# A long convolution with experts on one core: a Fourier transform without the filter's zero taps, and the experts' second product with its weights stationary

## The chip, the cores and the metric

The kernel runs on one core of a Trainium2 chip. The metric is device time in microseconds. The engines are TensorE (PE; its weight loads are shown as PEld), VectorE (DVE), ScalarE (ACT), GpSimd (POOL) and SyncE (SP), which here only issues DMAs. Each engine takes its instructions in the order in which they are written in the program; engines wait for one another by semaphores.

## The reference

There are B = 2 sequences of S = 12480 tokens with D = 128 channels. A small network makes a filter from position embeddings, a window exp(-0.01 pos) damps it, and the product u = x * v is convolved with it causally along the tokens (by a Fourier transform of length 2 S). The result times x goes, token by token, through experts of 2048 hidden units with a rational function.

```python
h_filt = (np.maximum(pos_emb @ w1, 0.0) @ w2) * np.exp(-0.01 * pos)[:, None]
u = x * v
y = irfft(rfft(u, n=2 * S) * rfft(h_filt, n=2 * S))[:, :S]
x = (x * y).reshape(B * S, D)
h = x @ w_in                                   # (24960, 2048)
P = a[0] + a[1] * h + a[2] * h**2 + a[3] * h**3
Q = 1.0 + abs(b[0]) * abs(h) + abs(b[1]) * h**2
out = (P / (Q + 1e-6)) @ w_out                 # (24960, 128)
```

All data are float32 (w_in, w_out and the scalars arrive as float64 and are converted in the kernel).

## The kernel before

A token n is written as n = 128 m + n2: 98 blocks m of 128 residues n2. The transform of length L = 24960 = 195 * 128 is taken in two stages, for some channels at a time: over the blocks m for each residue (s1, a matmul with f1, to K1 = 98 frequencies), a rotation by twiddles on VectorE and GpSimd, then over the residues (s2, with dft). There the spectrum is multiplied with the filter's, and s3 goes back over the residues (with idft). The last step back, from the K1 frequencies to the blocks m, is done later, per residue, in attn_a (with the constants g).

**First part.** The filter network runs over groups of residues (hf_w, hf_t, hf_1, hf_2; 98 rows m each), and meanwhile the expert weights are converted. Then a loop over 32 groups of CG = 4 channels makes the filter's spectrum (stored to h_d) and the convolution of batch 0 (stored to y_d). Per group VectorE makes two products of 784 elements for the filter's twiddles (L160, L161), four sums of 392 (L543 to L546), two products of 784 for the input's twiddles (L160, L161) and two for the spectrum (L192, L193); GpSimd makes the sums of these (L166, L167, L195, L196) and ys (L568, L569).

**Second part.** The tokens are taken in 52 tiles of 5 residues (490 tokens; the last tile of each half batch has 4 residues, 392 tokens). A tile has four steps (c = 0 to 3) of 4 blocks of 128 hidden units (NWF = 4). In a step s the work of several steps is in flight, in this written order (from the loop at L987):

```python
run(s, act_q, 0); run(s, act_v, 0); run(s + 1, mm1, 0); run(s - 2, dve_e); slot(s, 0)
run(s, dve_v, 0); run(s, act_q, 1); run(s - 1, act_ln); run(s - 3, mm2); run(s - 2, dve_n); slot(s, 1)
run(s, act_v, 1); run(s, act_sq); run(s + 1, mm1, 1); run(s, dve_v, 1); run(s - 1, act_exp); run(s - 2, dve_g); slot(s, 2)
```

mm1 is the first product (two halves of 6 passes in fast float32, L844 to L846). ScalarE makes q (L854) and v (L863) from its result in PSUM, per half, then a square of q (L887), a logarithm (L891) and an exponential (L894) over whole steps. VectorE makes v (L873) per half and, over whole steps, e (L899), n (L904) and g (L908). mm2 (L922) is the second product: the tokens' values g are the stationary side, 128 tokens at a time, and the rows of w_out move, so that the sums come out with the tokens on the partitions, 4 chunks by 4 blocks a step. At the end of a tile store copies the sums from PSUM (L933, L936) and issues some 8 DMAs (L944).

Beside that, each call of slot places one further matmul group on TensorE: attn_a (half a tile's residues: the last step back of the transform, then x times it on VectorE, L796), attn_b (transposes, then ScalarE's ahi, L814, and VectorE's alo, L815, the input of the next tile) or, in the free slots, the next step of batch 1's convolution, two channels at a time: s1 (taken up by L154 on VectorE, then L166, L167 on GpSimd), s2 (L188, then L195, L196), s3 (ScalarE's L205). What a slot's matmuls made is taken up (take_up) only in the next call of slot, and all share one PSUM buffer (cv). A tile has 12 slots; ATTN gives those for attn_a, attn_a, attn_b: (1, 2, 4) beside the convolution, (1, 3, 5) without. The free slots take s1, s2, s3 in turn.

The product u for batch 1 is made by GpSimd (L230) in four quarters of 32 channels, 8 pieces each, two pieces per slot (load_step); all quarters use one buffer, so that a quarter begins after the last s1 of the one before. READY says how many slots after the last piece s1 may begin: 5 for the first quarter, 2 for the others. GpSimd first clears two rows (L225).

## Time and profile before

| | before |
|---|---|
| median of 3 runs | 2547.77 us (2546.77 to 2547.78) |
| span of the profiled execution | 2545.4 us |
| profiled execution's own time | not listed apart from its span; the median lies 2.4 us above the span |
| VectorE busy | 2411.3 us, 95% |
| TensorE busy, its weight loads | 2180.8 us, 86%; 1829.2 us, 72% |
| ScalarE busy | 2103.6 us, 83% |
| GpSimd busy | 561.5 us, 22% |
| second product L922 | 6656 passes, 833.2 us busy |

The engines' busy time over the span, in 40 equal slices of 64 us, each digit a share in tenths (9 is 90% or more):

```
DVE  8999997799999998999899999999999999999997
ACT  6311121899999997999899999999999999999996
POOL 3466656222242224124321200000000000000000
```

The first seven slices are the first part, the next sixteen have batch 1's convolution beside the experts (GpSimd's work ends with it), the rest are experts alone. In the timeline rows below the first number is the start in us from the beginning of the span, the second the duration; then engine, line, operation, output and inputs, shapes, count, and in brackets how long the engine was idle before and for whom it waited. Instructions of one engine overlap a little in the records, so that the distance between two starts says better than the duration what an instruction costs a full engine.

### The profile page before, as it was taken

How to read it: one execution, taken by the hardware profiler on the slowest of the kernel's cores; microseconds unless marked ns; L12 is line 12 of the kernel's file. 1: busy time of each engine (PE TensorE's matmuls, PEld its weight loads, DVE VectorE, ACT ScalarE, POOL GpSimd, SP SyncE). 2: the span in 40 equal slices, each digit the busy share in tenths (PEclk: the TensorE clock that was granted, in tenths of full speed). 3: DMA queues.
4: the chain of work that ended last, by engine and by line, in shares of the span. 5: the costliest groups of instructions: out<-in, count | busy, mean ns of one | idle time of the engine just before them, and what ended most of it. 6: DMA issues, size and time to landing. Idle time of an engine off the chain costs nothing.

```text
span 2545.4 us, 33926 instructions
## 1 busy us (share of the span) xinstructions
PE 2180.8 (86%) x13344; PEld 1829.2 (72%) x13344; DVE 2411.3 (95%) x1945; ACT 2103.6 (83%) x1919; POOL 561.5 (22%) x522
## 2 busy tenths in 40 slices
PE   6888888789989998999899989888888898888877
PEld 4666665678877877788788767667776777776665
DVE  8999997799999998999899999999999999999997
ACT  6311121899999997999899999999999999999996
POOL 3466656222242224124321200000000000000000
PEclk9999989899999999999999999999999999999999
DMA  7444422822162235222322121111111111111100
GB/s 157 95 112 112 112 74 98 139 68 61 44 117 54 53 68 99 55 73 46 72 75 53 49 49 45 32 40 31 44 44 22 41 44 44 45 30 31 40 11 13
DMA packets 366001, 158.68 MB, mean 62 GB/s; under 512 B 299508, under 2 KB 347256, under 8 KB 362696
## 3 DMA queue, kind: packets, MB, share of 16 engines
q1 hardware_dynamic: 358696, 130.56, 23.2%
q10 hardware_dynamic: 7136, 25.86, 3.1%
q8 instruction: 107, 1.75, 0.3%
q14 instruction: 62, 0.51, 0.1%
HBM read 105.06 MB, written 51.31 MB: 61 GB/s over the span
## 4 chain that ended last, share of the span: by engine, by line
ACT 34%; DVE 30%; PE 21%; issue 9%; POOL 2%; DMA 1%; SPq 1%; ACTq 0%; DVEq 0%; POOLq 0%
ACT r L891 9%; ACT r L894 9%; ACT q L854 8%; PE acc L922 7%; DVE v L908 6%; ACT v L863 5%; DVE r L904 3%; DVE q L899 3%; PE cv L201 3%; PE cv L202 2%; DVE ta L188 2%; DVE v L873 2%; DVE tb L161 2%; PE cv L142 2%; DVE zh L544 2%
## 5 line engine op out<-in xcount | busy, mean ns | idle before, releaser
L922 PE MATMUL acc<-wout,v 128*128 128x128 f32 (+2 forms) x6656 | 833.2, 284 | 59.2 <-DVE v L908 35.2
L922 PEld LDWEIGHTS acc<-wout,v 128*128 128x128 f32 (+2 forms) x6656 | 790.6, 193 | 111.4 <-DVE v L908 55.3
L863 ACT ACTIVATE v<-h,sc 128x980 f32<-128x980 f32 (+1 forms) x416 | 683.2, 1642 | 8.0 <-PE acc L922 8.0
L854 ACT ACTIVATE q<-h 128x980 f32<-128x980 f32 (+1 forms) x416 | 613.7, 1559 | 6.4 <-PE h L846 6.4
L873 DVE SCALAR_TENSOR_TENSOR v<-v,sc,h 128x980 f32<-128x980 f32 (+1 forms) x416 | 504.9, 1214 | 59.7 <-ACT v L863 57.6
L887 ACT ACTIVATE q<-q,sc 128x1960 f32<-128x1960 f32 (+1 forms) x208 | 516.2, 2482 | 0.0
L891 ACT ACTIVATE r<-q,sc 128x1960 f32<-128x1960 f32 (+1 forms) x208 | 515.0, 2476 | 0.2 <-DVE v L908 0.2
L894 ACT ACTIVATE r<-r 128x1960 f32<-128x1960 f32 (+1 forms) x208 | 497.1, 2390 | 0.0
L899 DVE SCALAR_TENSOR_TENSOR q<-q,sc,r 128x1960 f32<-128x1960 f32 (+1 forms) x208 | 467.3, 2247 | 4.9 <-ACT r L894 1.1
L908 DVE SCALAR_TENSOR_TENSOR v<-v,sc,r 128x1960 f32<-128x1960 f32 (+1 forms) x208 | 465.5, 2238 | 0.1
L844 PE MATMUL h<-ahi,win_l 128*128 128x490 f32 (+1 forms) x832 | 365.0, 439 | 100.9 <-DVE v L873 98.5
L904 DVE SCALAR_TENSOR_TENSOR r<-q,r 128x1960 f32<-128x1960 f32 (+1 forms) x208 | 450.7, 2167 | 0.1
L845 PE MATMUL h<-alo,win_h 128*128 128x490 f32 (+1 forms) x832 | 320.6, 385 | 0.0
L846 PE MATMUL h<-ahi,win_h 128*128 128x490 f32 (+1 forms) x832 | 318.1, 382 | 0.0
L844 PEld LDWEIGHTS h<-ahi,win_l 128*128 128x128 f32 x832 | 158.5, 191 | 158.8 <-DVE v L873 133.3
L195 POOL TENSOR_TENSOR yy<-ta 128x196 f32<-128x196 f32 x64 | 122.1, 1908 | 368.3 <-DVE ta L188 368.3
L846 PEld LDWEIGHTS h<-ahi,win_h 128*128 128x128 f32 x832 | 158.7, 191 | 26.4
L845 PEld LDWEIGHTS h<-alo,win_h 128*128 128x128 f32 x832 | 159.4, 192 | 16.0 <-DVE alo L815 0.4
L790 PE MATMUL cv<-yc,gt 98*98 98x128 f32 x1004 | 130.9, 277 | 32.4 <-DVE an L796 29.9
L790 PEld LDWEIGHTS cv<-yc,gt 98*98 98x98 f32 x1004 | 115.0, 165 | 52.1 <-DVE an L796 48.6
L205 ACT ACTIVATE ys<-cv 98x512 f32<-98x512 f32 x64 | 76.9, 1202 | 76.2 <-PE cv L202 76.2
L201 PE MATMUL cv<-idft,yy 128*98 128x256 f32 x256 | 80.6, 396 | 57.3 <-DVE ta L188 33.1
(109 smaller groups left out, 2574.5 us busy)
## 6 DMA issues: line engine op xcount, KB each, us to landing
yc<-y_d SPq DMA_DIRECT2D x23, 980.0 KB
gt<-in_g_dram SPq DMA_DIRECT2D x48, 375.2 KB
h_d<-hg ACTq DMA_DIRECT2D x32, 392.0 KB
y_d<-ys ACTq DMA_DIRECT2D x16, 784.0 KB
hg<-h_d SPq DMA_DIRECT2D x64, 196.0 KB
y_d<-ys SPq DMA_DIRECT2D x16, 784.0 KB
xq<-in_x_dram SPq DMA_DIRECT2D x32, 196.0 KB
vq<-in_v_dram SPq DMA_DIRECT2D x32, 196.0 KB
```

The lines of the kernel that those rows point to most:

```text
L844: nc.tensor.matmul(out=t[:, k, 0:w], lhsT=wl, rhs=hi[:, 0:w], start=True, stop=False)
L845: nc.tensor.matmul(out=t[:, k, 0:w], lhsT=wh, rhs=lo[:, 0:w], start=False, stop=False)
L854: nc.scalar.activation(out=halves(st_q[s], i, width(s)), in_=st_h[s, i], func=AF.Abs, **({} if short else {"scale": col("b0")}))
L863: nc.scalar.activation(out=v, in_=st_h[s, i], func=AF.Square, bias=col("s"))
L873: stt(out=v, in0=v, scalar=col("k"), in1=h, op0=ALU.add, op1=ALU.mult)
L887: nc.scalar.activation(out=whole(st_q, s), in_=whole(st_q, s), func=AF.Square, bias=col("dl"))
L891: nc.scalar.activation(out=whole(st_r, s), in_=whole(st_q, s), func=AF.Ln, **({"bias": col("ka")} if short else {}))
L894: nc.scalar.activation(out=whole(st_r, s), in_=whole(st_r, s), func=AF.Exp, scale=-1.0)
L899: nc.vector.scalar_tensor_tensor(out=q, in0=q, scalar=col("ka") if short else 0.0, in1=whole(st_r, s), op0=ALU.add, op1=ALU.mult)
L904: nc.vector.scalar_tensor_tensor(out=r, in0=whole(st_q, s), scalar=2.0, in1=r, op0=ALU.subtract, op1=ALU.mult)
L908: nc.vector.scalar_tensor_tensor(out=v, in0=v, scalar=col("p0" if short else "a0"), in1=whole(st_r, s), op0=ALU.add, op1=ALU.mult)
L922: nc.tensor.matmul(out=acc[j][0:k, q // 128, :], lhsT=g[:, i, q:q + k], rhs=wout[:, f, :], start=(f == 0 and q == 0), stop=(f == NF - 1), ...
```

## The change

The window exp(-0.01 n) is zero in float32 from token 10398 on, so that many filter taps are left out. With TAPS = 10398 the filter has MF = 82 blocks for 98, the transform's length need only be S + TAPS - 1, which gives N1 = 179 blocks for 195, L = 22912, and K1 = 90 frequencies for 98. All tiles with K1 in their shape shrink by that; the filter network runs over 82 rows. The loads of pos_emb are cut in rows 0 to 79 and 80, 81.

In mm2 a block of w_out is now stationary and the step's 490 tokens move, so that the sums come out with the channels on the partitions (one bank of 490 columns). mm2 is called in two halves. At the tile's end collect copies the sums to SBUF; two slots of the next tile (o0 and o1) transpose them back, 3 and 2 residues at a time, and their takes copy them from PSUM by ScalarE; after the second two DMAs store the tile, with the 5 residues of a block of tokens side by side (2560 bytes). A step has four slots; SLOTS gives what stands in the 16 of a tile, and two ("") stay empty. The loads for the tile after next are asked for in slot 8.

```diff
-L = 2 * S
-N1 = L // N2
-K1 = 98
+WINDOW = np.exp(np.float32(-0.01) * np.arange(S, dtype=np.float32))
+TAPS = int(np.flatnonzero(WINDOW)[-1]) + 1
+MF = min(M, -(-TAPS // N2))
+N1 = -(-(S + TAPS - 1) // N2) // 2 * 2 + 1
+L = N1 * N2
+K1 = (N1 + 1) // 2
...
-ATTN = ((1, 2, 4), (1, 3, 5))
+SLOTS = ({1: "a0", 3: "a1", 5: "b", 8: "", 11: "", 13: "o0", 15: "o1"},
+         {1: "a0", 4: "a1", 7: "b", 13: "o0", 15: "o1"})
...
-            load_rows(t[:, 0:NPL], pos_emb, H2 + p0, NPL, 0, FO, True)
-            load_rows(t[:, NPL:], pos_emb, H2 - p0 - NPL, NPL, 0, FO, True)
+            for o, t0 in ((0, H2 + p0), (NPL, H2 - p0 - NPL)):
+                    for r0, r1 in ((0, MF // 16 * 16), (MF // 16 * 16, MF)):
+                        nc.sync.dma_start(out=t[r0:r1, o:o + NPL], in_=rows(pos_emb, r0, r1 - r0, t0, NPL, 0, FO))
...
-        def mm2(s):
-                acc[j] = accp.tile([128, 4, D], F32, tag="acc", name="acc")
-            for i in range(NWF):
-                f = NWF * c + i
-                for q in range(0, w, 128):
-                    k = min(128, w - q)
-                    nc.tensor.matmul(out=acc[j][0:k, q // 128, :], lhsT=g[:, i, q:q + k], rhs=wout[:, f, :], ...)
+        def mm2(s, i):
+                acc[j] = accp.tile([128, 512], F32, tag="acc", name="acc")
+            for k in range(2 * i, 2 * i + 2):
+                f = NWF * c + k
+                nc.tensor.matmul(out=acc[j][:, 0:w], lhsT=wout[:, f, :], rhs=st_v[s][:, k, 0:w], ...)
...
-        def store(j):
-            nc.scalar.activation(out=t[:, 0:full, :], in_=a[:, 0:full, :], func=AF.Identity)
-                nc.scalar.activation(out=t[0:k, full, :], in_=a[0:k, full, :], func=AF.Identity)
-            while p < w:
-                    nc.sync.dma_start(out=ob[...], in_=t[...])
+        def collect(j):
+            ot[j] = mp.tile([128, NPT * M], F32, tag="ot", name="ot", bufs=1)
+            nc.scalar.activation(out=ot[j][:, 0:w], in_=acc.pop(j)[:, 0:w], func=AF.Identity)
+        def store(j, q):
+            def fill(cv):
+                for i in range(i0, i1):
+                    nc.tensor.transpose(out=cv[0:M, 0, (i - i0) * D:(i - i0 + 1) * D], in_=t[:, i * M:(i + 1) * M],
+                                        identity=ident)
+            def take(cv):
+                nc.scalar.activation(out=o[:, i0:i1, :].rearrange("p t c -> p (t c)"),
+                                     in_=cv[0:M, 0, 0:(i1 - i0) * D], func=AF.Identity)
+                if i1 == n:
+                    for r0, r1 in ((0, 96), (96, M if n0 < H2 else M - 1)):
+                        nc.sync.dma_start(out=..., in_=o[r0:r1, 0:n])
+            issue(fill, take)
...
+            what = at.get(i)
+            if what:
+                t = j - 1 if what[0] == "o" else j + 1
+                if 0 <= t < len(tiles):
+                    (store if what[0] == "o" else attn_a)(t, q) if what[1:] else attn_b(t)
+                    return
             take_up()
-            if i == at[2] + 1:
+            if i == 8:
                 load_xg(j + 2)
                 load_y(j + 2)
-            conv_step((i - sum(i > k for k in at)) % 3)
+            if what is None:
+                conv_step((i - sum(i > k for k in at)) % 3)
...
             run(s - 1, act_ln)
-            run(s - 3, mm2)
+            run(s - 3, mm2, 0)
+            slot(s, 1)
             run(s - 2, dve_n)
-            slot(s, 1)
             run(s, act_v, 1)
+            run(s - 3, mm2, 1)
+            slot(s, 2)
             run(s, act_sq)
             run(s + 1, mm1, 1)
             run(s, dve_v, 1)
             run(s - 1, act_exp)
             run(s - 2, dve_g)
-            slot(s, 2)
+            slot(s, 3)
             if s >= 3 and steps[s - 3][1] == NC - 1:
-                store(steps[s - 3][0])
+                collect(steps[s - 3][0])
+        for q in range(2):
+            store(len(tiles) - 1, q)
+        take_up()
```

## Rows read from the trace of the kernel before

**Rows 1.** Busy time by stretch: length, PE, PEld, DVE, ACT, POOL, clock, DMA
```profile
80.00:240.00 160.00, 134.56 (x637) 99.87 (x636) 156.74 (x177) 29.32 (x50) 97.38 (x83) 0.97 0.46 109
...
446.00:1481.00 1035.00, 932.70 (x5928) 809.22 (x5928) 967.72 (x667) 938.28 (x789) 304.30 (x291) 0.98 0.32 69
1489.00:2478.00 989.00, 830.55 (x5409) 710.05 (x5407) 974.20 (x621) 989.00 (x838) 0.00 (x0) 0.97 0.15 37
```

**Rows 2.** Timeline of ScalarE in the late stage, one tile
```profile
2441.84 2.33 ACT L933 ACTIVATE ot<-acc 128x384 f32<-128x384 f32 x1
2442.21 2.13 ACT L936 ACTIVATE ot<-acc 106x128 f32<-106x128 f32 x1
2442.37 2.85 ACT L854 ACTIVATE q<-h 128x980 f32<-128x980 f32 x1
...
2478.84 2.48 ACT L933 ACTIVATE ot<-acc 128x384 f32<-128x384 f32 x1
```

**Rows 3.** Timeline of ScalarE beside the convolution
```profile
854.38 0.57 ACT L814 ACTIVATE ahi<-cv 128x490 fp32r<-128x490 f32 x1
...
880.85 1.22 ACT L205 ACTIVATE ys<-cv 98x512 f32<-98x512 f32 x1 [0.99 <-PE cv L202]
881.84 1.04 ACT L854 ACTIVATE q<-h 128x980 f32<-128x980 f32 x1
882.78 1.92 ACT L891 ACTIVATE r<-q,sc 128x1960 f32<-128x1960 f32 x1
884.60 1.06 ACT L863 ACTIVATE v<-h,sc 128x980 f32<-128x980 f32 x1
885.56 1.92 ACT L887 ACTIVATE q<-q,sc 128x1960 f32<-128x1960 f32 x1
...
889.11 0.97 ACT L854 ACTIVATE q<-h 128x980 f32<-128x980 f32 x1
...
898.14 0.57 ACT L814 ACTIVATE ahi<-cv 128x490 fp32r<-128x490 f32 x1
```

**Rows 4.** Timeline of VectorE beside the convolution
```profile
877.82 0.97 DVE L188 TENSOR_TENSOR ta<-cv,hg 128x784 f32<-128x784 f32 x1
878.71 2.25 DVE L899 SCALAR_TENSOR_TENSOR q<-q,sc,r 128x1960 f32<-128x1960 f32 x1
880.87 1.23 DVE L873 SCALAR_TENSOR_TENSOR v<-v,sc,h 128x980 f32<-128x980 f32 x1
882.02 2.19 DVE L904 SCALAR_TENSOR_TENSOR r<-q,r 128x1960 f32<-128x1960 f32 x1
...
885.69 1.24 DVE L873 SCALAR_TENSOR_TENSOR v<-v,sc,h 128x980 f32<-128x980 f32 x1 [0.59 <-ACT v L863]
886.84 2.25 DVE L908 SCALAR_TENSOR_TENSOR v<-v,sc,r 128x1960 f32<-128x1960 f32 x1
889.01 0.55 DVE L796 TENSOR_TENSOR an<-cv,xt 98x384 f32<-98x384 f32 x1
```

**Rows 5.** Timeline of TensorE beside the convolution
```profile
878.85 0.67 PE L201 MATMUL cv<-idft,yy 128*98 128x256 f32 x2 [0.78 <-DVE ta L188]
...
882.89 3.72 PE L922 MATMUL acc<-wout,v 128*128 128x128 f32 x32
```

**Rows 6.** Groups by line: busy us, mean ns of one, idle before
```profile
L160 DVE TENSOR_TENSOR ta<-cs,tw 128x784 f32<-128x784 f32 x32 | 31.2, 974 | 1.1 <-POOL zu L167 0.2
L543 DVE TENSOR_TENSOR zh<-ta,tb 64x392 f32<-64x392 f32 x32 | 41.2, 1287 | 1.1
```

**Rows 7.** Timeline of TensorE in the first part, passes of 392 columns
```profile
319.33 0.82 PE L177 MATMUL cs<-zu,dft 128*128 128x392 f32 x2
319.99 0.82 PE L178 MATMUL cs<-zu,dft 128*128 128x392 f32 x2
```

**Rows 8.** Timeline of GpSimd and TensorE at the change to the third quarter
```profile
948.00 1.80 POOL L225 MEMSET uq<- 2x2048 f32 x1 [6.99 <-PE cv L142]
...
973.82 1.68 PE L142 MATMUL cv<-f,uq 98*128 98x196 f32 x4 [8.95 <-POOL uq L230]
```

More of the change, by code (lines that the diff above doesn't have):

```diff
@@ L77, in constants @@
     g = f(np.stack([np.cos(ga) * w, -np.sin(ga) * w * sg[None, :, None]], 2))
-    pos = np.arange(S, dtype=np.float32)
     win = np.zeros((M * N2,), np.float32)
-    win[:S] = np.exp(np.float32(-0.01) * pos)
-    win = win.reshape(M, N2)
+    win[:S] = WINDOW
+    win = win.reshape(M, N2)[:96]
     return {
@@ L137, in build, with s1_mm @@
     vb = [v[b] for b in range(B)]
-    def s1_mm(cvt, u, cl0, n):
+    def s1_mm(cvt, u, cl0, n, k=M):
         for c in range(n):
             nc.tensor.matmul(out=cvt[:, c // 2, c % 2 * 2 * K1:(c % 2 + 1) * 2 * K1],
-                             lhsT=u[:, cl0 + c, :], rhs=f1, start=True, stop=True)
+                             lhsT=u[0:k, cl0 + c, :], rhs=f1[0:k], start=True, stop=True)
     def pair(pool):
@@ L455, in build @@
         nb = H2 // NP
-        W = NP * M
+        W = NP * MF
         pT, rT = {}, {}
@@ L495, in hf_2 @@
             for p in range(NP):
-                nc.tensor.matmul(out=ps[0:M, p // 2, (p % 2) * 2 * D:(p % 2 + 1) * 2 * D],
-                                 lhsT=r[:, p * M:(p + 1) * M], rhs=bdw2, start=True, stop=True)
-            src = ps[0:M].rearrange("m b (p s c) -> m (b p) s c", p=2, s=2)
+                nc.tensor.matmul(out=ps[0:MF, p // 2, (p % 2) * 2 * D:(p % 2 + 1) * 2 * D],
+                                 lhsT=r[:, p * MF:(p + 1) * MF], rhs=bdw2, start=True, stop=True)
+            src = ps[0:MF].rearrange("m b (p s c) -> m (b p) s c", p=2, s=2)
             for q in range(D // UQ):
-                o = hf[q].rearrange("m c (s p) -> m p s c", s=2)[:, i * NP:(i + 1) * NP]
+                o = hf[q][0:MF].rearrange("m c (s p) -> m p s c", s=2)[:, i * NP:(i + 1) * NP]
                 a = src[:, :, :, q * UQ:(q + 1) * UQ]
@@ L578, in build @@
                 t = cvs()
-                s1_mm(t, hf[a // gq], a % gq * CG, CG)
+                s1_mm(t, hf[a // gq], a % gq * CG, CG, MF)
                 s1h_out(t, zh[a])
@@ L824, in second_part @@
         st_h, st_q, st_v, st_r = {}, {}, {}, {}
-        acc = {}
+        acc, ot, om = {}, {}, {}
         def width(s):
@@ L910, in dve_g @@
             del st_q[s], st_r[s]
-        def mm2(s):
+        def mm2(s, i):
             j, c = steps[s]
             w = width(s)
-            if c == 0:
-                acc[j] = accp.tile([128, 4, D], F32, tag="acc", name="acc")
-            g = st_v.pop(s)
-            for i in range(NWF):
-                f = NWF * c + i
-                for q in range(0, w, 128):
-                    k = min(128, w - q)
-                    nc.tensor.matmul(out=acc[j][0:k, q // 128, :], lhsT=g[:, i, q:q + k], rhs=wout[:, f, :],
-                                     start=(f == 0 and q == 0), stop=(f == NF - 1), skip_group_check=True)
@@ L948, in second_part @@
-        at = []
+            if c == 0 and i == 0:
+                acc[j] = accp.tile([128, 512], F32, tag="acc", name="acc")
+            for k in range(2 * i, 2 * i + 2):
+                f = NWF * c + k
+                nc.tensor.matmul(out=acc[j][:, 0:w], lhsT=wout[:, f, :], rhs=st_v[s][:, k, 0:w], start=(f == 0),
+                                 stop=(f == NF - 1))
+            if i == 1:
+                st_v.pop(s)
+        def collect(j):
+            w = tiles[j][2] * M
+            ot[j] = mp.tile([128, NPT * M], F32, tag="ot", name="ot", bufs=1)
+            nc.scalar.activation(out=ot[j][:, 0:w], in_=acc.pop(j)[:, 0:w], func=AF.Identity)
@@ L950, in slot @@
+        at = {}
         def slot(s, k):
@@ L956, in slot @@
             j, c = steps[s]
-            i = 3 * c + k
+            i = 4 * c + k
             if i == 0:
-                at[:] = ATTN[item[0] is None]
-            if j + 1 < len(tiles) and i in at:
-                q = at.index(i)
-                if q == 2:
-                    attn_b(j + 1)
-                else:
-                    attn_a(j + 1, q)
-                return
+                at.clear()
+                at.update(SLOTS[item[0] is None])
+            what = at.get(i)
+            if what:
+                q = int(what[1:] or 0)
+                t = j - 1 if what[0] == "o" else j + 1
+                if 0 <= t < len(tiles):
+                    (store if what[0] == "o" else attn_a)(t, q) if what[1:] else attn_b(t)
+                    return
             take_up()
-            if i == at[2] + 1:
+            if i == 8:
                 load_xg(j + 2)
                 load_y(j + 2)
-            conv_step((i - sum(i > k for k in at)) % 3)
+            if what is None:
+                conv_step((i - sum(i > k for k in at)) % 3)
         def run(s, fn, *args):
```

44 lines of the change are left out of this document (20 added, 24 removed).

## The prediction

> **What bounds the kernel now.** I read the busy shares first (VectorE 95%, ScalarE 83%, TensorE 86% of the span; front table), then the busy time by stage, because those shares are means over three stages. From 446 to 1481 us, where the convolution of batch 1 runs beside the experts, no engine is full: VectorE 967.7, ScalarE 938.3, TensorE 932.7 of 1035 us [rows 1]. From 1489 to 2478, experts alone, ScalarE is busy in all of 989.00 us and VectorE in 974.2 [rows 1]. The first part (to about 445) is VectorE's: 156.7 of 160 us between 80 and 240 [rows 1].
>
> Late stage: the timeline of ScalarE shows its instructions starting one behind the other, and a tile takes 37.00 us from one L933 to the next [rows 2]. What an instruction adds to that is its distance to the next start: 384 elements 0.37 us, 128 elements 0.16, that is 0.82 ns per element above some 0.055 [rows 2]. VectorE's steps of 2.16, 1.15, about 2.11, 1.15 and 2.17 (distances, as the recorded 1.23, 2.25 and 2.19 overlap by 0.08 [rows 4]) make 8.74 a step, 35.0 a tile and 36.3 with the input's three: it has 0.7 us of room, ScalarE none.
>
> Convolution stage: a tile takes 898.14 - 854.38 = 43.76 us [rows 3], and I take 43.7. What sets it is a ring, read from who waits for whom. TensorE's inverse product L201 starts when VectorE's ta of L188 is done (877.82 to 878.85: 1.03 [rows 4, 5]); ScalarE's copy L205 waits for it (at 880.85, 2.00 later, idle 0.99 [rows 3, 5]); then ScalarE's order is q, r, v (0.99, 0.94, 1.82 [rows 3]), v ends 1.09 after 884.60 and releases VectorE's L873 (idle 0.59 [rows 3, 4]); L873 and L908 take 1.15 and 2.17, and the next take-up stands at 889.01 [rows 4]. Sum 11.19, and that is the distance of 877.82 to 889.01. The second product, L922, is not in the ring: TensorE works it off beside it, 32 passes in 3.72 us, 3.55 without the tail of the last [rows 5].
>
> **The change, part by part.**
>
> *Shorter transform, first part.* The constants give 82 filter rows for 98, 179 blocks for 195, K1 = 90 for 98. A VectorE product over 784 elements becomes 720: 0.974 us now [rows 6], distance about 0.88; 64 elements at the 1.1 ns of 2.16 us / 1960 [rows 4] are 0.07. Six such per group make 0.42. The four L543 to L546 (392 to 360) take 1.287 at the worst [rows 6]; the row's long mean points to interference by GpSimd, so the gain lies between 4 x 0.035 and 4 x 0.11; I take 0.28. That is 0.70 x 32 groups = 22 us, between 18 and 28, all of it on the path, since VectorE hardly waits there [rows 1]. The fewer partitions of the filter network shorten no VectorE instruction; the added DMAs of its loads stand at the start, ahead of a queue with room: 0, at most +2.
>
> *Second product.* 64 products of 128 columns per tile, two passes each, become 16 of 490. The nearest row for a long float32 pass is 392 columns: two passes 0.66 apart at 319.33 and 319.99, 0.33 each [rows 7]; 490 gives 0.41, and a step 8 x 0.41 = 3.30 for 3.55. On TensorE a tile saves 1.0 us, and five transposes back, passes of 128 columns like today's of L922 (3.72 / 32 = 0.12 [rows 5]), cost 0.6. Neither is on the path by itself.
>
> *ScalarE.* L933 and L936 (0.37 + 0.16) become copies of 490, 384 and 256 elements: 0.46 + 0.37 + 0.27 by the slope of [rows 2]: +0.57, bounds 0.4 and 0.9 (if reading 98 partitions or the waits cost extra). Where ScalarE is full this is on the path: 29.75 tiles without convolution x 0.55 = +16. VectorE cannot be late there, it gains that much more room.
>
> *Order of the slots.* Per tile there are 16 slots for 12, 7 of them taken for 3: nine remain for the convolution as before, but the takes stand elsewhere, and one buffer (cv) serves all: a slot's matmuls wait for the take of the slot before. I followed one tile, steps c0 to c3, with the distances above. VectorE's own sum is 4 x 8.74 + 1.4 (input) + 6 x 0.82 (720 elements) = 41.3.
> c0: slots 0 to 3 hold s1, a0, s2, a1. VectorE's v waits 0.8 for ScalarE (reason under c3); a0 0.1. 11.8 us.
> c1: a1's take (0.48 with release), then s3 (2.0), then on ScalarE the copy ys (1.22 + 0.05), then b's transposes (TensorE must also finish the half product of 1.65 behind s3), 0.6, then ahi 0.57 and only then VectorE's alo: 5.2 us after a1's take began. VectorE has 0.33 + 1.15 + 2.11 = 3.6 to do meanwhile, so it stands 1.6. Today b's take lies after exp and g, with no such wait. 12.1 us.
> c2: s2's matmuls wait for s1's take at the end of c1 (24.0 after c0's start); 1.25, then 1.4 (first product), 1.65 (half of the second), 2.0 (s3): ys at 30.3, where ScalarE, behind its v, had been ready at 28.1. No wait on VectorE: 10.4.
> c3: ScalarE goes on from 30.3 without a gap, ys 0.96, squares 1.82, exp 1.73, the new copy 0.46, q 0.87, v 1.08: done 37.2, where VectorE, at 36.5, wants v: 0.8 lost. s3 is copied at the end of c3, behind exp, so the same lateness meets c0 again. 10.4.
> Sum 44.7 (41.3 + 1.6 + 0.8 + 0.9): one ring through all four steps, against 43.7: +1.0 x 22.25 tiles = +22. Bounds: 41.3 (no wait at all) to 46 (every take that stands close behind its matmuls waits another 0.3).
>
> *Where the convolution begins and ends.* Counted in the code: its first product now stands in slot 9 of 12 of tile 0, its last at 23.42 tiles; with 16 slots at 0.625 and 22.875. So 0.42 tiles fewer carry it, x (44.7 - 37.6) = -3.
>
> *Change of quarter.* A new quarter of u is used by TensorE at the earliest 5 slots after its first piece; a slot falls from 3.64 to 2.8 us, GpSimd's work does not shrink. Before the third quarter GpSimd starts at 948.00 and TensorE, idle for 8.95, goes on at 973.82 [rows 8]: 25.8 us. Counted in slots, today the second quarter has 8 (no wait), the third 5, the fourth 5; changed 5, 5 and 9: about 15.4 us of TensorE's order, hence a wait near 10, 10 and 0. Both of the first stop VectorE too: +17 for +13 today; and the very first quarter is asked for half a step earlier, +4. In all +7, bounds -5 and +18.
>
> *Rest.* One tile beside the convolution has four residues. Its steps are a fifth shorter on VectorE, 7 us of 35.0, which today's order can't use while TensorE also loads a last chunk of 8 columns per block, and the changed one can: -5, between -7 and 0. At the end two transposes and copies stand against six DMA issues less: -1, between -3 and +3. SP gets 2 stores for about 8 per tile. They now stand behind the last copy back, in slot 0 of the tile after next, and block what follows in SP's queue until ScalarE has made it; that is first the load of hg, wanted a whole group (some 15 us) later, so I cost it at nothing. The loads of x, the constants and y for the tile after next move from slot 5 of 12 to 8 of 16 and keep nine slots, 25 us, to the first product that reads them, for eight or 29 today; were they late, the wait would be those few microseconds once in two tiles (a chunk of y serves two).
>
> Sum: -22 + 16 + 22 - 3 + 7 - 5 - 1 = +14. The profiled span is 2545.4 us, the median of the runs 2547.77, so 2.4 lie around it: 2545.4 + 14 + 2.4, about 2561 us.
>
> **Rivals.**
> A, the other side: VectorE's sum sets the convolution stage. For it: VectorE has 967.7 of 1035 us there [rows 1], the largest; the finer halves could let TensorE deliver earlier than I place it. If all waits go, a tile is 41.3: -22 + 16 - 53 - 2 + 7 - 5 - 1 = -60, 2488; if today's waits of some two microseconds a tile stay and only VectorE's 0.4 are saved, the stage gives -9: -22 + 16 - 9 - 2 + 7 - 5 - 1 = -16, 2532. It decides from a tile under 44.1 on, where +22 has become +8. Against it: the wait for alo follows from the order of the queues. The Trainium skill speaks for it: its page "Perfetto Trace Analysis", section "Identifying the Most-Contended Engine", has the engine with the highest occupancy as the one to optimise, VectorE here, and this change lightens that one and loads another. By that rule the time would follow VectorE, down; the late rows, with ScalarE at 100% beside VectorE's 98.5%, agree only in part. Chance 0.22.
> B, cancellation: the late copies hide. They would need gaps on ScalarE, and [rows 2] show none; or the stages cancel by smaller errors. +14 - 16 = -2: 2546. Chance 0.15.
> C, more waits: a convolution tile of 46, or the long passes with their weights not hidden (0.2 x 8 a step on TensorE, which would then carry 38 + 6 us per tile): 22.25 x 2.3 = 51 in place of 22, 2591. This is also how the change could fail to make the product shorter. Chance 0.10.
>
> **Numbers.** Forecast 0.53, alone 2546 to 2576. Two parts in a thousand, 5 us, is about what a measurement tells from no change. Slower: the forecast less its lower edge (0.49) and C, 0.59. Within: B and that edge, 0.17. Faster: A and a little of B, 0.24. The range takes in B and A's upper end with some of what lies below, and part of C: 2525 to 2586.
>
> **What would show it.** Right: late tiles at 37.5 to 37.7 from collect to collect with ScalarE full; convolution tiles at 44 to 45.5 with a wait of VectorE's alo for ahi of one to two microseconds per tile; group period of the first part down by 0.7; L922's successor at 0.41 a pass; two TensorE waits for uq near 10. Wrong: convolution tiles under 43.7, no wait of alo, or a late tile that stays at 37.0.

## The result and the profile after

The changed kernel takes 2568.16 us (median of 4 runs, 2565.94 to 2568.62) beside 2547.27 for the kernel before (4 runs, 2545.42 to 2547.78): ratio 1.0077, 95% interval 1.0063 to 1.0092. It is slower by 20.9 us; the forecast was 2561 and slower. The profiled execution spans 2566.3 us after, 2545.4 before. Line numbers of the changed kernel are five to nine higher: L814 is L823, L815 L824, L205 L210, L142 L147, L543 to L546 are L552 to L555; the second product is L929, its collecting copy L937, the copies back L954.

Busy shares of the page after (engine, us, share, instructions), and busy time by stage (length; PE, PEld, DVE, ACT, POOL; clock; DMA share; GB/s), which answers to [rows 1]:

```profile
PE 2118.1 (83%) x8608; PEld 1393.3 (54%) x8608; DVE 2397.8 (93%) x1945; ACT 2120.1 (83%) x1971; POOL 645.0 (25%) x522
```

```profile
80.00:240.00 160.00, 134.11 (x671) 101.59 (x670) 156.32 (x188) 30.77 (x55) 100.01 (x88) 0.96 0.49 108
446.00:1481.00 1035.00, 891.13 (x3781) 612.08 (x3781) 952.45 (x656) 923.73 (x797) 391.81 (x288) 0.97 0.30 64
1500.00:2490.00 990.00, 804.07 (x2917) 478.03 (x2915) 964.63 (x612) 990.00 (x852) 0.00 (x0) 0.96 0.15 35
```

TensorE and VectorE are less busy than before in the middle stage (932.7 to 891.1, 967.7 to 952.5), and the stage is longer all the same. Late, ScalarE is still busy in every microsecond while VectorE has more room than before. So the change took work from engines that were not late and gave some to the one that was.

Where the time went, from the starts of the copy ahi (L814, L823), one a tile, in the two traces; the last column puts the forecast's terms together (-22; 22 - 3 + 7 - 5; 16 - 1):

```
                       before     after    change  forecast
first ahi at           444.81    430.66     -14.2      -22
... to tile 25        1073.8    1094.8      +21.0      +21
... to the end        1026.8    1040.9      +14.0      +15
```

Tile times, ahi to ahi, of tiles 0 to 26 (tile 12 is the short one; the convolution ends in tile 24):

```
tile       0    1    2    3    4    5    6    7    8    9   10   11   12   13
before  18.3 41.1 43.3 43.7 43.7 43.7 44.4 43.9 43.7 43.7 43.8 43.7 48.6 44.0
after   15.4 42.8 46.6 44.5 44.5 44.5 54.4 44.5 44.5 44.5 46.1 46.1 48.8 42.0
tile      14   15   16   17   18   19   20   21   22   23   24   25   26
before  43.2 43.7 43.7 43.9 49.6 43.7 43.7 43.7 43.7 43.8 41.5 34.1 33.5
after   43.6 46.1 44.5 46.6 44.5 44.5 44.5 44.5 44.5 45.1 37.6 34.6 34.1
```

*Late stage.* ScalarE's timeline after (start, duration, engine, line), the counterpart of [rows 2]:

```profile
2311.16 2.31 ACT L937 ACTIVATE ot<-acc 128x490 f32<-128x490 f32 x1
...
2348.81 2.46 ACT L937 ACTIVATE ot<-acc 128x490 f32<-128x490 f32 x1
2349.28 2.87 ACT L863 ACTIVATE q<-h 128x980 f32<-128x980 f32 x1
...
2354.74 2.42 ACT L954 ACTIVATE om<-cv 98x384 f32<-98x384 f32 x1
2355.12 3.87 ACT L896 ACTIVATE q<-q,sc 128x1960 f32<-128x1960 f32 x1
...
2360.49 2.33 ACT L954 ACTIVATE om<-cv 98x256 f32<-98x256 f32 x1
2360.76 2.95 ACT L863 ACTIVATE q<-h 128x980 f32<-128x980 f32 x1
```

Read the distances to the next start: 0.47, 0.38, 0.27, in all 1.12 where L933 and L936 had 0.53. A tile is 2348.81 - 2311.16 = 37.65 for 37.08 (mean of eight tiles before), so 0.57 of these 0.59 us are paid.

*Beside the convolution.* VectorE's waits in one tile after (723.25 to 767.71: engine, line, waited for; us, times, longest), and busy time in that tile:

```profile
DVE alo L824 <- ACT ahi L823: 1.5, 1, 1.5
DVE v L882 <- PE h L855: 0.5, 1, 0.5
DVE q L908 <- ACT r L903: 0.4, 1, 0.4
```

```profile
723.25:767.71 44.46, 39.12 (x171) 26.77 (x171) 41.77 (x29) 40.74 (x36) 15.90 (x12) 1.00 0.22 58
```

The 1.5 us come about as follows, on TensorE, ScalarE and VectorE of another tile:

```profile
900.44 1.81 PE L929 MATMUL acc<-v,wout 128*128 128x490 f32 x4
902.09 0.59 PE L818 MATMUL cv<-ident,an 98*128 98x98 f32 x5
```

```profile
900.64 1.11 ACT L210 ACTIVATE ys<-cv 90x512 f32<-90x512 f32 x1 [1.53 <-PE cv L207]
901.54 1.03 ACT L872 ACTIVATE v<-h,sc 128x980 f32<-128x980 f32 x1
902.71 0.58 ACT L823 ACTIVATE ahi<-cv 128x490 fp32r<-128x490 f32 x1
```

```profile
903.33 0.67 DVE L824 TENSOR_TENSOR alo<-cv,ahi 128x490 fp32r<-128x490 f32 x1 [1.54 <-ACT ahi L823]
```

ScalarE stood 1.53 us for the inverse product, half a second product (1.65 for four passes, 0.41 each) ran ahead of the transposes, ahi came behind them, and VectorE, with nothing else to do in its order, waited for ahi. Before, VectorE's waits in a tile were 1.8 us, all for ScalarE's v. The second line of the waits names TensorE's h, but ScalarE's q had read that h two us earlier; ScalarE's v, which the same instruction needs, ended at 752.10, and L882 started at 752.13, so that this is a wait for ScalarE too.

*Change of quarter.* TensorE's timeline after, at the first products of the first and second quarter, answering to [rows 8]:

```profile
461.37 1.57 PE L147 MATMUL cv<-f,uq 98*128 98x180 f32 x4 [10.01 <-POOL uq L235]
...
706.30 1.57 PE L147 MATMUL cv<-f,uq 98*128 98x180 f32 x4 [6.94 <-POOL uq L235]
```

The other two waits are 5.2 and 3.1; before they were 4.1, none, 8.9 and 3.6.

*Tiles 2, 10 and 15.* Tiles 10 and 15 are 1.6 longer than the steady 44.46 and tile 2 is 2.1 longer, and no quarter changes there. Below are tile 10 and a stretch in it (columns as for the stages above; the clock is the number before the DMA share), then TensorE's instruction just before that stretch:

```profile
856.64:902.71 46.07, 40.73 (x171) 27.86 (x171) 41.86 (x29) 40.74 (x35) 13.86 (x12) 0.96 0.28 67
863.50:866.90 3.40, 3.40 (x9) 2.46 (x8) 3.40 (x4) 2.78 (x2) 2.65 (x4) 0.50 0.06 16
```

```profile
862.11 0.57 PE L182 MATMUL cv<-zu,dft 128*128 128x180 f32 x2 [1.90 <-DVE ta L159]
```

The granted clock is 1.00 in the steady tiles, and in this stretch it was 0.50, the lower of its two levels (1.2 of 2.4 GHz); passes of the first product started 0.41 us apart in place of 0.22. Tiles 2 and 15 have such a stretch too, all three right behind a wait of 1.9 us for VectorE's ta. That wait stands in each steady tile of the changed kernel; the longest of TensorE in a steady tile was 1.1 before and is 1.2 in e1 below, and none of their steady tiles lost clock. What lets the clock fall in these three tiles and not in the others, no run shows.

*First part.* Groups by line from 100 to 300 us, VectorE after (count, busy us, mean ns, idle before), against [rows 6], and then the first of the four sums before, in the same stretch:

```profile
L552 DVE TENSOR_TENSOR zh<-ta,tb 64x360 f32<-64x360 f32 x20 | 31.5, 1577 | 0.7
L553 DVE TENSOR_TENSOR zh<-ta,tb 64x360 f32<-64x360 f32 x19 | 27.3, 1436 | 0.6
L165 DVE TENSOR_TENSOR ta<-cs,tw 128x720 f32<-128x720 f32 x20 | 18.2, 908 | 0.6
```

```profile
L543 DVE TENSOR_TENSOR zh<-ta,tb 64x392 f32<-64x392 f32 x19 | 30.6, 1609 | 0.7
```

The six products fell as the forecast had it (974 to 908 ns). The first two of the four sums hardly did: before they took 1609 and 1469 ns. Their timeline beside GpSimd's shows why they might not:

```profile
206.59 1.63 DVE L552 TENSOR_TENSOR zh<-ta,tb 64x360 f32<-64x360 f32 x1
208.25 1.49 DVE L553 TENSOR_TENSOR zh<-ta,tb 64x360 f32<-64x360 f32 x1
209.77 0.53 DVE L554 TENSOR_TENSOR zh<-ta,tb 64x360 f32<-64x360 f32 x1
210.33 0.53 DVE L555 TENSOR_TENSOR zh<-ta,tb 64x360 f32<-64x360 f32 x1
```

```profile
206.57 1.26 POOL L577 TENSOR_TENSOR ys<-qt 90x512 f32<-90x512 f32 x1
207.79 1.55 POOL L578 TENSOR_TENSOR ys<-qt 90x512 f32<-90x512 f32 x1
```

Four sums of one size: the two that run beside GpSimd's L577 and L578 take three times as long as the two that run alone.

### The profile page after: what moved, and what is told of

Its sections match the earlier page's. It is cut to its first block, busy times and chain, and to the rows that moved or that the text cites. A ratio compares the mean times of both kernels' runs of the same rounds, so it can differ in the third digit from the quotient of the medians.

```text
span 2566.3 us, 24007 instructions
## 1 busy us (share of the span) xinstructions
PE 2118.1 (83%) x8608; PEld 1393.3 (54%) x8608; DVE 2397.8 (93%) x1945; ACT 2120.1 (83%) x1971; POOL 645.0 (25%) x522
## 5 line engine op out<-in xcount | busy, mean ns | idle before, releaser
L929 PE MATMUL acc<-v,wout 128*128 128x490 f32 (+1 forms) x1664 | 778.3, 597 | 64.8 <-DVE v L917 40.6
L863 ACT ACTIVATE q<-h 128x980 f32<-128x980 f32 (+1 forms) x416 | 622.7, 1566 | 20.2 <-PE h L855 15.8
L882 DVE SCALAR_TENSOR_TENSOR v<-v,sc,h 128x980 f32<-128x980 f32 (+1 forms) x416 | 504.8, 1213 | 26.5 <-ACT v L872 15.4
L900 ACT ACTIVATE r<-q,sc 128x1960 f32<-128x1960 f32 (+1 forms) x208 | 521.5, 2507 | 0.0
L903 ACT ACTIVATE r<-r 128x1960 f32<-128x1960 f32 (+1 forms) x208 | 498.8, 2398 | 0.0
L853 PE MATMUL h<-ahi,win_l 128*128 128x490 f32 (+1 forms) x832 | 387.0, 465 | 125.3 <-DVE v L882 124.6
L929 PEld LDWEIGHTS acc<-v,wout 128*128 128x128 f32 x1664 | 309.7, 199 | 329.9 <-issue 211.6
L171 POOL TENSOR_TENSOR zu<-ta 128x180 f32<-128x180 f32 x64 | 115.9, 1811 | 445.9 <-DVE ta L159 445.9
L799 PEld LDWEIGHTS cv<-yc,gt 90*98 90x98 f32 x1004 | 117.5, 165 | 76.7 <-ACT om L954 37.2
L799 PE MATMUL cv<-yc,gt 90*98 90x128 f32 x1004 | 130.9, 277 | 32.4 <-ACT om L954 16.1
L200 POOL TENSOR_TENSOR yy<-ta 128x180 f32<-128x180 f32 x64 | 114.6, 1790 | 145.4 <-DVE ta L193 144.3
L210 ACT ACTIVATE ys<-cv 90x512 f32<-90x512 f32 x64 | 71.3, 1115 | 88.8 <-PE cv L207 88.7
```

The lines of the kernel that those rows point to most:

```text
L853: nc.tensor.matmul(out=t[:, k, 0:w], lhsT=wl, rhs=hi[:, 0:w], start=True, stop=False)
L863: nc.scalar.activation(out=halves(st_q[s], i, width(s)), in_=st_h[s, i], func=AF.Abs, **({} if short else {"scale": col("b0")}))
L882: stt(out=v, in0=v, scalar=col("k"), in1=h, op0=ALU.add, op1=ALU.mult)
L900: nc.scalar.activation(out=whole(st_r, s), in_=whole(st_q, s), func=AF.Ln, **({"bias": col("ka")} if short else {}))
L903: nc.scalar.activation(out=whole(st_r, s), in_=whole(st_r, s), func=AF.Exp, scale=-1.0)
L929: nc.tensor.matmul(out=acc[j][:, 0:w], lhsT=wout[:, f, :], rhs=st_v[s][:, k, 0:w], start=(f == 0), stop=(f == NF - 1))
```

## Experiments

Ten more kernels ran beside the kernel before; the time is the median of 4 to 11 executions. "First ahi" is the start of the first copy ahi, which ends the first part; "steady" is a tile beside the convolution away from the changes of quarter, "late" one without the convolution.

```
run                  us      ratio to before, 95%       first ahi  steady  late
before            2547.3                                 444.81    43.7   37.1
after             2568.2    1.0077 [1.0063, 1.0092]      430.66    44.5   37.65
e1_transform      2521.3    0.9897 [0.9882, 0.9912]      428.65    43.5   37.1
e2_product        2590.8    1.0170 [1.0156, 1.0183]      446.40    44.9   37.7
e5_order          2542.4    0.9977 [0.9968, 0.9986]      430.26    44.3   37.1
e3_dve_copy       2549.3    1.0005 [0.9996, 1.0014]      429.74    44.3   37.0
e4_ready          2554.6    1.0032 [1.0020, 1.0044]      429.15    44.5   37.6
e6_bslot          2587.3    1.0160 [1.0146, 1.0174]      429.83    45.3   37.6
e7_sums           2557.6    1.0038 [1.0025, 1.0052]      422.12    44.5   37.6
e8_best           2509.0    0.9853 [0.9839, 0.9866]      422.60    43.5   37.1
e9_mult           2504.4    0.9832 [0.9818, 0.9845]      416.08    43.5   37.1
e10_copy          2500.9    0.9818 [0.9804, 0.9831]      417.21    43.5   36.9
```

### e1_transform: the shorter transform alone

The kernel before with all that the diff has on the transform, whose core is below; product, stores and three slots a step stay.

```
-L = 2 * S
-N1 = L // N2
-K1 = 98
...
+MF = min(M, -(-TAPS // N2))
+N1 = -(-(S + TAPS - 1) // N2) // 2 * 2 + 1
+L = N1 * N2
+K1 = (N1 + 1) // 2
...
-                s1_mm(t, hf[a // gq], a % gq * CG, CG)
+                s1_mm(t, hf[a // gq], a % gq * CG, CG, MF)
```

> Only the shorter transform is taken over: the second product, its stores and the three slots of a step are those of the kernel before. Theory (the two halves of the change pull in opposite directions; the transform's half is all gain): the first spectrum of the experts' input still comes some 14 us earlier, a tile beside the convolution falls by 0.1 to 0.5 us (720 elements for 784 in VectorE's takes, on the ring), late tiles stay at 37.1; in all 2547 - 14 - 22 x 0.3 - 2 for fewer waits at the quarters = about 2525, between 2515 and 2535. Rival (the halves cancel for another reason: the shorter transform itself makes a tile of the convolution longer, because its takes reach the shared buffer at another moment): tile above 43.9, total above 2538.

Measured 2521.27, 26 us faster than before: the theory holds, the rival does not. Its steady tile, busy time and VectorE's waits:

```profile
835.45:878.93 43.48, 40.05 (x262) 34.54 (x262) 41.50 (x30) 40.55 (x36) 10.10 (x12) 1.00 0.24 56
```

```profile
DVE v L881 <- ACT v L871: 2.0, 3, 0.7
```

VectorE does 41.50 us of work where the kernel before had 41.91, but waits 2.0 for 1.8: of the 0.41 saved, 0.28 reach the tile (43.48 for 43.76).

### e2_product: the second product and its order alone

The reverse: `mm2`, `collect`, `store`, `SLOTS` and the loop of the steps from the changed kernel, the long transform of the kernel before. Its edit against the changed kernel, the constants standing for the rest:

```
-N1 = -(-(S + TAPS - 1) // N2) // 2 * 2 + 1
-L = N1 * N2
-K1 = (N1 + 1) // 2
+L = 2 * S
+N1 = L // N2
+K1 = 98
```

> Only the second product with its transposes back and the four slots of a step are taken over; the transform is the long one of the kernel before. Theory (the product's half is all loss): late tiles 37.65 for 37.1 (+14 in 26 tiles), a tile beside the convolution 44.9 to 45.5 (+1.2 to +1.8 over before, x 22), the first part as before: 2547 + 14 + 27 = 2588, between 2578 and 2600. Rival (the product's half is neutral and the transform's effect on the quarters makes the loss): 2550 to 2570, tile at most 44.2.

Measured 2590.79, 43.6 us slower, steady 44.9, late 37.7. The theory holds. The two halves add up: -26.0 + 43.6 = +17.6 for +20.9 measured, with some 4 us of uncertainty on each term.

### e5_order: the order of slots with the old product

On the changed kernel:

```
-SLOTS = ({1: "a0", 3: "a1", 5: "b", 8: "", 11: "", 13: "o0", 15: "o1"},
-         {1: "a0", 4: "a1", 7: "b", 13: "o0", 15: "o1"})
+SLOTS = ({1: "a0", 3: "a1", 5: "b", 8: "", 11: "", 13: "", 15: ""},
+         {1: "a0", 4: "a1", 7: "b", 13: "", 15: ""})
...
-                nc.tensor.matmul(out=acc[j][:, 0:w], lhsT=wout[:, f, :], rhs=st_v[s][:, k, 0:w], start=(f == 0),
-                                 stop=(f == NF - 1))
+                for q in range(0, w, 128):
+                    k = min(128, w - q)
+                    nc.tensor.matmul(out=acc[j][0:k, q // 128, :], lhsT=g[:, i, q:q + k], rhs=wout[:, f, :],
+                                     start=(f == 0 and q == 0), stop=(f == NF - 1), skip_group_check=True)
...
-                collect(steps[s - 3][0])
+                store(steps[s - 3][0])
```

> The changed kernel with the second product of before (64 products of 128 columns a tile, its two copies and its stores), but in the changed order of 16 slots a tile, the product cut into two halves, the last two slots left empty. It tells the order of the slots from the product. Theory (beside the convolution the order makes the waits, the product's own copies only a little): late tiles 37.1, a tile beside the convolution 44.0 to 44.6 with VectorE's alo still waiting 1.2 to 1.8 us for ahi; in all 2568 - 15 for the late tiles - 22 x 0.2 = 2549, between 2541 and 2557. Rival (the copies and transposes of the product lengthen the tile, the order costs nothing): tile 43.4 to 43.6 as with the shorter transform alone, total near 2532.

Measured 2542.44, steady 44.29, late 37.1. VectorE's waits in one tile (809.97 to 854.26):

```profile
DVE alo L824 <- ACT ahi L823: 1.7, 1, 1.7
DVE q L908 <- ACT r L903: 0.6, 1, 0.6
DVE v L882 <- ACT v L872: 0.3, 1, 0.3
```

The theory holds. With nothing of the new product in it, the tile is 0.8 longer than e1's and has the wait for ahi. It hands no more through the shared buffer cv than e1 does, three groups for the next tile and nine of the convolution; what differs is where the 16 slots stand and that the product is cut into two halves, and no run takes these two apart. So, with the medians: the transform -26.0 (2547.2 to 2521.3), the order +21.2 (to 2542.4), the product with its copies +25.7 (to 2568.2). Of the last, 14.8 fall from tile 24 on, where ScalarE is full and the product's copies are what it has more of, and 9.2 beside the convolution: 0.2 in each steady tile, the rest unevenly (tiles 1, 10, 12 and 15 are longer than e5's, 6 and 11 shorter).

### e3_dve_copy: the copies back on VectorE

```
-                nc.scalar.activation(out=o[:, i0:i1, :].rearrange("p t c -> p (t c)"),
-                                     in_=cv[0:M, 0, 0:(i1 - i0) * D], func=AF.Identity)
+                nc.vector.tensor_copy(o[:, i0:i1, :].rearrange("p t c -> p (t c)"), cv[0:M, 0, 0:(i1 - i0) * D])
```

> The changed kernel with its two copies behind the transposes back (384 and 256 elements per tile) on VectorE in place of ScalarE; the copy that collects the sums stays on ScalarE. Theory (late tiles are the sum of ScalarE's instructions, the added copies cost what they last): a late tile loses up to 0.37 + 0.27 = 0.64 us on ScalarE, until VectorE's own sum of about 36.3 + 0.7 = 37.0 decides; so 37.0 to 37.2 for 37.65, about -13 over 26 tiles; beside the convolution, where a ring with waits decides, -0.5 to +0.7 a tile. In all 2568 - 13 + 0 = 2555, between 2545 and 2565. Rival (VectorE's occupancy, 93% of the span and the highest, sets the time): each copy of VectorE is paid in full, 0.7 a tile x 52 = 36, total near 2590 to 2604.

Measured 2549.3, 18.9 us less than the changed kernel; late tiles 37.0: the theory holds. The same stretch in the changed kernel, and then here:

```profile
1500.00:2470.00 970.00, 787.10 (x2850) 467.51 (x2849) 945.42 (x599) 970.00 (x836) 0.00 (x0) 0.96 0.15 35
```

```profile
1500.00:2470.00 970.00, 797.58 (x2910) 477.91 (x2908) 969.28 (x663) 969.57 (x796) 0.00 (x0) 0.97 0.15 35
```

VectorE takes on 24 us there, and the time falls: that decides against the rival that VectorE's occupancy sets it (2590 to 2604). Rival A of the prediction is about the stage beside the convolution, where a steady tile of this run is:

```profile
769.06:813.40 44.34, 39.32 (x171) 26.84 (x171) 42.30 (x31) 40.14 (x34) 15.90 (x12) 1.00 0.26 62
```

VectorE does 0.5 us more in it than the 41.77 of the changed kernel, and the tile is 0.1 shorter: VectorE's sum does not set that stage either. The Trainium skill's page "Perfetto Trace Analysis", section "Identifying the Most-Contended Engine", takes the engine with the highest occupancy as the one to optimise first. Over the whole span that is VectorE, and this run gave it more work and gained; over the late stage alone it is ScalarE, and there the trace agrees. Now both engines are full, so another copy can't be moved for nothing.

### e4_ready: later first products of the quarters

```
-READY = (5, 2)
+READY = (8, 5)
```

> The changed kernel with the first product of each quarter of the convolution asked for three slots of the order later (8 slots behind the first piece of u in place of 5, and 5 in place of 2 behind the last). Theory (the wait of TensorE for u at a change of quarter stops VectorE too, a slot passed over costs nothing but a later end of the convolution): the tile with 54.4 us falls to 46 or less, the waits of TensorE for the products u, 25 us in sum, go to under 8; the convolution ends up to one tile later, and a tile beside it is 6.8 us longer than one without: 2568 - 17 + 6 = 2557, between 2548 and 2564. Rival (what is waited for is GpSimd's work on u, which VectorE's tile passes anyway; later slots only move the loss): 2566 to 2572.

The two numbers are the slots left between the last piece of u and the first product of the first quarter, and of the later ones, not of the first and the last piece, as the expectation puts it; "three slots later" is right for both. Measured 2554.63, 13.5 us less than the changed kernel; tile 6 falls from 54.4 to 46.3 (the theory had 46 or less), and all that is left of the waits for u (engine, line; us, times, longest) is:

```profile
PEld cv L147 <- POOL uq L235: 3.5, 1, 3.5
```

The convolution ends a tile later (tile 24 takes 45.0 for 37.6). The waits were a loss of their own and not only GpSimd's work showing up somewhere: the theory holds but for these 0.3 us.

### e6_bslot: the input's transposes one slot later

```
-SLOTS = ({1: "a0", 3: "a1", 5: "b", 8: "", 11: "", 13: "o0", 15: "o1"},
+SLOTS = ({1: "a0", 3: "a1", 5: "", 6: "b", 11: "", 13: "o0", 15: "o1"},
```

> The changed kernel with the transposes of the next tile's input one slot later beside the convolution (slot 6 for 5; the empty slot 8 goes to 5, so that nine slots stay for the convolution). The take of ahi and alo then lies behind VectorE's v and g steps, as in the kernel before. Theory (the tile is VectorE's sum of 41.3 plus the waits, and each wait taken away shortens it): alo's wait of 1.57 us falls under 0.3, a tile beside the convolution from 44.5 to 42.9 to 43.5; in all 2568 - 22 x 1.3 = 2539, between 2532 and 2550. Rival (the ring goes through ScalarE and the shared buffer, and the wait only moves to the next take): tile 44.0 to 44.6, total 2558 to 2570.

Measured 2587.3, 19 us slower than the changed kernel: my theory falls. Busy time and VectorE's waits in a tile (774.20 to 819.54):

```profile
774.20:819.54 45.34, 39.40 (x170) 26.75 (x170) 42.04 (x30) 40.65 (x36) 13.78 (x12) 1.00 0.30 68
```

```profile
DVE v L882 <- ACT v L872: 0.8, 1, 0.8
DVE q L908 <- ACT r L903: 0.7, 1, 0.7
DVE alo L824 <- ACT ahi L823: 0.6, 1, 0.6
DVE v L882 <- PE h L855: 0.5, 1, 0.5
DVE ta L193 <- issue: 0.5, 1, 0.5
```

The wait for ahi did fall, from 1.5 to 0.6, and others took its place: 3.1 us in all for 2.4. Even the rival's upper end (44.6, 2570) was too low. The run moves two slots at once, so it doesn't tell which of them made it worse; that a wait named in the trace can be taken away and the tile still grow is what it shows.

### e7_sums: GpSimd's two sums of the first part on VectorE

```
...
-            engines[0].tensor_tensor(out=dst[:, 1:3], in0=a, in1=b, op=ALU.add)
-            engines[1].tensor_tensor(out=dst[:, 0:4:3], in0=a, in1=b, op=ALU.subtract)
+            def sums():
+                nc.vector.tensor_tensor(out=dst[:, 1:3], in0=a, in1=b, op=ALU.add)
+                nc.vector.tensor_tensor(out=dst[:, 0:4:3], in0=a, in1=b, op=ALU.subtract)
+            return sums
...
```

What s3p_out returns here is called in the next group, behind the four sums of the filter.

> The changed kernel with GpSimd's two sums of 512 elements per group in the first part (the inverse transform's output, 1.26 and 1.55 us) made by VectorE, behind its four sums of the filter. It tests why those four sums, 1.6, 1.5, 0.53 and 0.53 us for one size, got only 0.13 shorter together with 360 for 392 elements. Theory (the first two are long because GpSimd's two instructions run at the same time, and these don't depend on the transform's length): the first two sums fall to 0.53 to 0.6 each, VectorE gets two of some 0.75 more, a group from 10.3 to 9.6 to 9.9, in all 2568 - 32 x 0.55 = 2550, between 2545 and 2557. Rival (the first two are long of themselves, because they are the first to read what VectorE has just written): they stay at 1.5 and more, a group takes 11.5 to 11.8, total 2605 to 2616.

Measured 2557.58, 10.6 us less than the changed kernel, for the 18 expected. VectorE and GpSimd in one group:

```profile
203.94 0.91 DVE L165 TENSOR_TENSOR ta<-cs,twh 128x720 f32<-128x720 f32 x1 [0.59 <-POOL zu L172]
...
205.70 0.53 DVE L552 TENSOR_TENSOR zh<-ta,tb 64x360 f32<-64x360 f32 x1
206.26 0.53 DVE L553 TENSOR_TENSOR zh<-ta,tb 64x360 f32<-64x360 f32 x1
...
208.01 0.69 DVE L578 TENSOR_TENSOR ys<-qt 90x512 f32<-90x512 f32 x1
```

```profile
201.72 2.19 POOL L172 TENSOR_TENSOR zu<-ta,tb 128x360 f32<-128x360 f32 x1
```

All four sums now take 0.53: the long ones were long because of GpSimd's instructions, which the change leaves at 512 elements. That settles the cause. The Trainium skill, page "SBUF — State Buffer", section "SBUF: two separate sides", says that a VectorE instruction with two inputs from SBUF and a GpSimd instruction that reads SBUF exclude each other, the later one standing still until the earlier has ended; the trace agrees (1.63 and 1.49 against 0.53). What is missing is the same thing the other way round: zu on GpSimd has moved beside VectorE's product L235 and takes 2.19 for 0.82, and VectorE then waits 0.59 for it, 13.1 us in all groups for 0.5 in the changed kernel.

### e8_best, e9_mult and e10_copy: towards a faster kernel

e8 is e1 with the edit of e7 and three more slots before the third and the fourth quarter:

```
-READY = (5, 2)
+READY = (5, 2, 5, 5)
...
-                return lambda: len(us) > g // gq and us[g // gq][1] == 0 and us[g // gq][2] >= READY[g >= gq]
+                return lambda: len(us) > g // gq and us[g // gq][1] == 0 and us[g // gq][2] >= READY[g // gq]
```

> What the runs so far point to, on the kernel with the shorter transform alone (2521): the two sums of the first part on VectorE as in the run beside it, and the first product of the third and the fourth quarter asked for three slots later, since TensorE waits 8.9 and 3.6 us for u there and the tiles take 48.2 and 48.5 for 43.5. Theory: -18 for the sums, -9.7 for the two waits, +4.3 because the convolution ends two thirds of a tile later: 2521 - 23 = 2498, between 2490 and 2508. Rival (the sums are long of themselves, and a later quarter only moves its loss): 2521 + 40 = 2561.

Measured 2508.98, 12.3 less than e1 for the 23 expected. The first ahi comes 6.1 us earlier than in e1 (in e7 it came 8.5 earlier than in the changed kernel; the expectation, made before e7 had run, had 18); the two quarters' tiles fall from 48.2 and 48.5 to 42.1 and 44.0, while the convolution goes on into tile 25.

e9 is e8 with the product u of the first part on GpSimd:

```
-                mult_u(nc.vector)
+                mult_u(nc.gpsimd)
```

> The kernel of the run before (2509) with the product u of the first part (97 x 512, 1.03 us in some 22 groups) on GpSimd in place of VectorE. There VectorE now waits 0.6 us a group for GpSimd's zu, which takes 2.19 us instead of 0.82 while that product runs beside it. Theory (the two hold each other up whenever both work from SBUF alone): VectorE's 1.03 + 0.6 go from a group, TensorE's 8.7 of 10.1 us and new collisions with VectorE's own sums give some back: a group 9.0 to 9.4, 2509 - 22 x 0.9 = 2489, between 2480 and 2500. Rival (GpSimd's added work collides with VectorE's six sums and takes back all): 2503 to 2520.

Measured 2504.36, 4.6 less for the 20 expected: neither the theory's 2480 to 2500 nor quite the rival. VectorE and GpSimd in one group:

```profile
202.50 0.53 DVE L551 TENSOR_TENSOR zh<-ta,tb 64x360 f32<-64x360 f32 x1
203.06 1.49 DVE L552 TENSOR_TENSOR zh<-ta,tb 64x360 f32<-64x360 f32 x1
```

```profile
202.55 1.62 POOL L234 TENSOR_TENSOR hu<-xq,vq 97x512 f32<-97x512 f32 x1
```

The collision took back 0.96 of the 1.03 moved; what is left comes from the shorter wait for zu (0.18 for 0.60). The first ahi comes 6.5 us earlier than in e8; that only 4.6 of them reach the end is not explained by a run.

e10 is e9 with the small copy of the old store, 106 x 128, on VectorE:

```
-                nc.scalar.activation(out=t[0:k, full, :], in_=a[0:k, full, :], func=AF.Identity)
+                nc.vector.tensor_copy(t[0:k, full, :], a[0:k, full, :])
```

> The kernel of the run beside it with the small copy of the experts' sums (106 x 128, 0.16 us on ScalarE, one in a tile) on VectorE. Theory (late tiles are ScalarE's sum, VectorE has room): a late tile 36.9 for 37.1, beside the convolution no change: 4 us less than the kernel beside it, between 2 and 7 less. Rival (VectorE's sum is the bound in either stage): the copy of some 0.25 us is paid in both, 12 us more.

Measured 2500.88, 3.5 us less than e9, late tiles 36.93 for 37.08: 0.16 us, ScalarE's price of that copy [rows 2]. The steady tile did not change. Busy time late:

```profile
1500.00:2430.00 930.00, 782.44 (x5119) 667.37 (x5118) 923.25 (x612) 930.00 (x766) 0.00 (x0) 0.97 0.15 34
```

This kernel beats both: 0.9818 of the kernel before, 67 us under the changed one, and it keeps the old second product.

## Why the prediction was right, step by step

The sign, the place of each loss and the total (2561 forecast, 2568 measured, inside the forecast's own 2546 to 2576) came out. Part of the agreement is luck: the stage beside the convolution came out at +21.0 for +21, but its terms (order, begin and end, quarters, short tile) were off by -4, -4, +6 and +2, which cancel. Slips in the working move it by about 1 us each: 2545.4 + 14 + 2.4 is 2561.8, 17 - 13 + 4 at the quarters is 8 and was put at 7, and 41.3 + 1.6 + 0.8 + 0.9 is 44.6 beside the 44.7 of the four steps. Point by point:

- *Shorter transform, first part: -22 forecast, -14.2 measured.* This is the term that was mis-sized, outside its own 18 to 28; its 7.8 us are as much as the 7 by which the total is off. A group fell by 0.52 (first to last L543 327.13 us, first to last L552 310.92, over 31 groups), not 0.70. The products' 0.42 was right. The four sums gave 0.13, the lower bound of the forecast (4 x 0.035), where I took 0.28: I had named GpSimd's interference and still let the long instructions shrink with their size. The 1.287 of [rows 6], which I took for the worst, is a mean: L543 takes 0.56 in some groups and 1.66 in most. e7 shows that the interference is made of GpSimd's instructions, whose size does not depend on the transform. The start is 1.6 later besides (first L552 at 86.31, first L543 at 84.69), where VectorE waits 2.8 for the filter network's tokens, loaded in more pieces, for 0.8 before; the forecast had 0 to +2 for it. That the loads make this wait was not tried alone.
- *ScalarE's copies: +16.* 0.57 a tile for 0.55, +14.0 to the end. e3 takes them off ScalarE and gets it back; e10 does the same with one of 0.16.
- *Second product: 0.41 a pass for the long form, nothing on the path.* 1.65 for four passes, right; TensorE's busy time in the middle stage fell by 41.6 us (5.1 of it by the transform: 927.6 in e1) and bought nothing: with the long passes and their copies the tile is 0.2 longer than e5's.
- *Order of the slots: +22.* A steady tile of 44.5 for 43.7, where I had 44.7 for 43.7; over tiles 1 to 23 that is +17.7. The wait of alo for ahi is 1.54, forecast 1.6. The two at the ends of the ring are 0.4 and 0.5, forecast 0.8 and 0.9 (the first falls on q, one instruction ahead of v, and waits for ScalarE's exponential L903); VectorE's own sum is 41.8, not 41.3. Two errors that in part cancel within the tile. Against e1's 43.5, e5 shows that the order makes 0.8 of it and the new product with its copies 0.2. But the forecast's picture of a sum and separate waits is only good for adding up: e6 took one away and the tile grew.
- *Begin and end of the convolution: -3.* Tile 0 is 2.9 shorter and tile 24 3.9: -6.8.
- *Change of quarter: +7, bounds -5 and +18.* What tiles 1 to 23 have beyond 0.77 each is +10, and the two tiles of the short step (12 and 13) lie 3.3 under it, so about +13 is left. Of this 5.7 lie in tiles 2, 10 and 15, where no quarter changes and the clock fell; the forecast has no term for the clock. What remains, some 8, is close to +7, but the waits are not those forecast: TensorE's are 10.0, 6.9, 5.2 and 3.1, where I had the second and third near 10 and the fourth at 0. e4 shows that they cost time.
- *Short tile: -5.* About -3, from tiles 12 and 13. *Tail: -1.* -0.4.
- *Rivals.* A needed tiles under 44.1 and no wait for alo; neither came, and e3's steady tile refutes the mechanism. B and C missed: the late copies do not hide, the tile did not reach 46.

## What to carry to other kernels

A change that makes the busiest engine lighter is worth what the stage's own ring gives: here the transform was worth 26 us, and another order of issue, with the same number of handovers through the shared buffer, took 21 back. Why this order makes the tile longer is shown only in part: shortening its largest wait (e6) did not help. Price each instruction that is added to an engine without gaps at its full distance to the next start, and look for an engine with room in that stage first. Where one of two equal instructions is three times as long, look at what runs beside it before scaling it with its size.

## What the runs showed of the hardware

Collisions between VectorE and GpSimd move when work is moved: 1.63 and 1.49 for 0.53 us on VectorE (changed kernel), then 2.19 for 0.82 on GpSimd (e7), then 1.49 for 0.53 on VectorE again (e9). In e9 a product of 1.03 us on VectorE, moved to an engine that is idle for more than half of the time, cost VectorE 0.96 us of standing still.

The granted clock of TensorE fell from 1.00 to 0.50 in three tiles of the changed kernel away from the changes of quarter, each time right behind a wait of 1.9 us, and such a tile was 1.6 us longer or more. The same wait stands in the tiles where the clock stayed at 1.00.
